# Experts in the order of their loads, with a slot count for each place, in a fused attention and mixture-of-experts kernel

## The chip, the core and the metric

The kernel runs on one core of one Trainium2 chip. The metric is the device time of one execution in microseconds (us), told as the median of three runs. A profile of one further execution shows the instructions of five engines: TensorE (PE for matmuls and transposes, PEld for its weight loads), VectorE (DVE), ScalarE (ACT), GpSimd (POOL) and SyncE (SP), which issues most DMAs. DMAs move data between DRAM and SBUF; matmuls write to PSUM, which has eight banks of 128 partitions by 512 fp32 numbers.

## The reference

All data are fp32. There are S = 2048 tokens of D = 448 features, H = 16 heads of 28, E = 8 experts with F = 1792 hidden features, and every token takes the two experts with the largest logits.

```python
def _A_ref(x, wqkv, wo):                       # attention
    q, k, v = (x @ wqkv).reshape(B, S, 3, H, Dh).transpose(2, 0, 3, 1, 4)
    p = softmax(einsum("bhqd,bhkd->bhqk", q, k) * Dh ** -0.5)
    return einsum("bhqk,bhkd->bhqd", p, v).transpose(0, 2, 1, 3).reshape(B, S, D) @ wo

def _B_ref(x, w_gate, w1, w2):                 # experts
    logits = x @ w_gate
    topk_idx = argsort(-logits)[:, :2]
    gates = softmax(take_along_axis(logits, topk_idx))
    out = 0
    for e in range(E):
        w = (gates * (topk_idx == e)).sum(-1, keepdims=True)
        out = out + w * (silu(x @ w1[e]) @ w2[e])
    return out

g = sigmoid((x * gate_w).sum(-1, keepdims=True))
return g * _A_ref(x, wqkv, wo) + (1 - g) * _B_ref(x, w_gate, w1, w2)
```

The inputs are random numbers with a spread of 0.05. How many tokens an expert gets (its load) is known only once the logits are computed. A load is about 512 on average (4096 choices over 8 experts).

## The kernel before

**Precision.** Each fp32 factor of a large product is split into a high half that TensorE takes in one pass (type fp32r) and a low half, the remainder; a product is the sum of high x high, high x low and low x high. ScalarE writes the high half as a copy, and VectorE or GpSimd subtracts it for the low one. The 448 features are four blocks of rows: three of 128, and a fourth of 64 rows that holds high and low halves together. So a product over the features takes 3 x 3 + 2 = 11 matmuls.

**Stages.** (1) After `BUSY` = 20 transposes of the identity (L338) with which PE begins, the value stage (to L388) goes through sixteen tiles of 128 tokens: PE makes the values and the logits of a tile, ScalarE copies the values to `v_s` (L376), and SP stores them in DRAM (L382). From the fifth tile on it also stores blocks of zeros from SBUF (`zf`) to `ys_d` (L385, L388): 24 blocks for spilled slots and one for the tail of each expert, 32 in all. (2) The query and key stage: `qk_tile` (L558) makes a block of 128 features of queries or keys for four chunks of 512 tokens; ScalarE copies the result to `hi` (L578), DVE subtracts (L581), SP stores both halves (L582, L583). Between DVE's pieces of this work stand those of `routing` (L397), a generator: top-two choice, each token's rank in its expert by matmuls with a triangle of ones (L431 to L433), the slot of each choice, and the lists `idx_i` (which token sits in a slot), `spill_i`, `cnt_i` (the loads) and `coef`. Four blocks come before the last piece of the routing, then three more (5, 2, 6); ahead of these three, the tokens of the first expert are gathered (`gather`, L202, an indirect DMA of GpSimd) and its first three weight tiles loaded (`load_w1`, L214, three DMAs each on SP). (3) The experts, L834 to L950. (4) Attention proper, L1040 on, whose exponentials run on ScalarE, then the output projection with the experts' rows gathered from `ys_d`.

**Slots.** Every expert has `CAP` = 576 slots, four tiles of 128 and a fifth of 64, and `CPAD` = 640 rows of `ys_d`. Tokens beyond 576 go to spill tiles of 128, which a loop at the end (L752) works off if there are any. Experts are taken in the order 0 to 7.

**Inside an expert.** The hidden features go in two halves (`hf`) of seven blocks. In the up layer each block is made for two halves of the columns (`HC` = 288 slots), 11 matmuls each (L870), so a half expert has 154 of them. ScalarE applies silu from PSUM: once to `hh` (the high half), once to `hf32` for GpSimd's low half (L749), and to `ht` for the fifth tile. In the second layer (L920) a tile of 128 slots takes 21 matmuls of 448 columns; before the four tiles stands the fifth (`last_slots`, L794), in a branch (L904) that is taken where the load is over 512. The first half's result waits in `ysb`, the second adds to it and stores to `ys_d`. Weights: SP loads `w1` (`load_w1`) and `w2` (`fetch_w2`) some tiles ahead; ScalarE splits off the high halves (L696, L734), GpSimd the low ones (L702, L740). `turn_x` (L718) transposes the next expert's gathered tokens, in the second halves.

**The score-maximum stream.** Attention needs each row's largest score. PE computes the scores for it among the experts' matmuls, in steps of six banks (`max_stream`, L91; matmuls L106, VectorE's reductions L126), and seven where the spare one of the two accumulator banks is lent (L120). The function `worked(ns, due, bank)` is called after every matmul of the experts with its length as the author reckons it. A step is emitted where a position is due: five dues in a half's up layer, six in the second halves of the last four experts, one at the fifth tile, and one in each of the four tiles.

```python
w1_due = [(18, 46, 73, 100, 128), (11, 35, 59, 83, 107, 131)]   # matmul of 0..153
W2_DUE = [(15, 13, 12, 10), (16, 14, 13, 12)]                    # matmul of 1..21, by tile
free = due <= i < due + 4 and (n_k > 1 or not turns)             # a bank may be lent
```

A finished maximum of four query tiles is transposed on PE and stored (`store_max`, L141), where a bank is free.

**Who sets the order.** PE, VectorE and ScalarE, and GpSimd too in the experts, run in the order in which the code is written. The order of SP's DMAs is made by a planner, which places them by its own estimate of when they can go; it is not the written one. For example, keys for the attention (L638), written in the seventh expert, are issued at 160.7 us, in the first.

## Time and profile before

| what | us |
| --- | --- |
| three runs | 1445.17, 1443.89, 1442.52 |
| median | 1443.89 |
| the profiled execution, its own time | 1443.26 |
| its span, first to last instruction | 1441.4 |
| PE busy / PEld busy | 1423.7 / 953.7 |
| DVE / ACT / POOL busy | 794.5 / 899.2 / 646.5 |
| expert stage | 121.8 to 913.9 |

How to read it: times count from the start of the span. In a row of busy time, `L870 PE MATMUL acc<-xeh,w1h 128*128 128x288` is a matmul of line 870 with the tile `xeh` as its input and `w1h` as its other one, into `acc`, over 288 columns. `[2.47 <-DVE dl L424]` says that the engine stood idle for 2.47 us before this instruction, and that what ended it was VectorE's write of `dl` on line 424. A row of waits, `ACT v_s L376 <- DMA v_d<-v_s: 14.1, 8, 4.6`, gives who waited for whom, then the total in us, how often, and the longest one. The granted clock is the share of its full clock that TensorE was given; it is 1.00 in all of this profile. PE's busy times overlap one another, so a matmul's cost is read from the distance between starts.

### The profile page before, as it was taken

The numbers are of one execution on the slowest core, as the hardware profiler recorded it, in microseconds if no ns is written. First come the engines' busy times: TensorE is split into PE (matmuls) and PEld (weight loads), VectorE is DVE, ScalarE is ACT, GpSimd is POOL, SyncE is SP. The second block draws the span as 40 slices with busy tenths as digits, with TensorE's granted clock in tenths as the row PEclk, the third lists the DMA queues.
The fourth block names the chain that finished last, engine by engine and source line by source line (L and its number), as shares of the span: only waits on it lengthen the run. The fifth ranks groups of instructions, "written<-read, shape, count | busy, mean of one in ns | idle before, by whom it ended". The sixth has DMA issues, their size and how long they took to land. (4 is left out here: it accounts for less than half of the span.)

```text
span 1441.4 us, 28118 instructions
## 1 busy us (share of the span) xinstructions
PE 1423.7 (99%) x11025; PEld 953.7 (66%) x11025; DVE 794.5 (55%) x858; ACT 899.2 (62%) x1559; POOL 646.5 (45%) x685
## 2 busy tenths in 40 slices
PE   9999999999999999999999999999999999999998
PEld 8788888888888888788888887533333333333347
DVE  5636777777778778778688787111142111221136
ACT  5235355344443553453444434799999999999981
POOL 1124597577666874874775656212222112112110
PEclk9999999999999999999999999999999999999999
DMA  9887532344133323331431320311422231142103
GB/s 332 291 289 238 169 112 78 97 136 129 43 103 118 103 81 110 123 98 55 137 118 37 107 70 3 108 47 49 130 55 59 78 98 47 43 122 64 32 20 119
DMA packets 110201, 153.18 MB, mean 106 GB/s; under 512 B 17884, under 2 KB 81516, under 8 KB 110064
## 3 DMA queue, kind: packets, MB, share of 16 engines
q1 hardware_dynamic: 100832, 129.86, 28.7%
q0 software_dynamic: 9088, 21.22, 4.9%
q8 instruction: 90, 1.47, 0.4%
q14 instruction: 47, 0.39, 0.1%
q10 hardware_dynamic: 144, 0.23, 0.1%
HBM read 109.20 MB, written 37.85 MB: 102 GB/s over the span
## 5 line engine op out<-in xcount | busy, mean ns | idle before, releaser
L126 DVE TENSOR_REDUCE mp<-pm 128x2 f32<-128x1024 f32 (+2 forms) x324 | 552.3, 1747 | 130.8 <-PE pm L106 130.3
L1058 ACT ACTIVATE P<-ps 128x1536 f32<-128x1536 f32 x254 | 367.9, 1448 | 0.0
L1067 PE MATMUL po<-P,V 128*32 128x512 f32 x2032 | 270.6, 604 | 0.0
L870 PE MATMUL acc<-xeh,w1l 128*128 128x288 f32 x880 | 258.5, 301 | 0.0
L870 PE MATMUL acc<-xeh,w1h 128*128 128x288 f32 x880 | 256.6, 298 | 0.0
L667 PEld LDWEIGHTS ps<-Q,Kh 29*128 29x128 f32 x2032 | 77.8, 183 | 212.6 <-ACT P L1057 212.3
L740 POOL TENSOR_TENSOR w2l<-w2r,w2h 128x448 fp32r<-128x448 f32 x112 | 129.0, 1153 | 168.9 <-ACT w2h L734 168.9
L870 PE MATMUL acc<-xel,w1h 128*128 128x288 f32 x660 | 195.1, 296 | 0.0
L667 PE MATMUL ps<-Q,Kh 29*128 29x512 f32 x2032 | 190.0, 444 | 0.0
L872 ACT ACTIVATE hh<-acc 128x288 fp32r<-128x288 f32 x224 | 92.3, 412 | 154.1 <-PE acc L870 154.1
L870 PEld LDWEIGHTS acc<-xeh,w1l 128*128 128x128 f32 x880 | 165.9, 189 | 18.6 <-issue 18.6
L920 PE MATMUL acc<-w2h,hh 128*128 128x448 f32 x448 | 171.8, 383 | 0.0
L870 PEld LDWEIGHTS acc<-xeh,w1h 128*128 128x128 f32 x880 | 165.7, 188 | 9.0 <-issue 7.3
L920 PE MATMUL acc<-w2l,hh 128*128 128x448 f32 x448 | 167.2, 373 | 0.0
L920 PE MATMUL acc<-w2h,hl 128*128 128x448 f32 x448 | 165.0, 368 | 0.0
L702 POOL TENSOR_TENSOR w1l<-w1r,w1h 128x512 fp32r<-128x512 f32 (+1 forms) x88 | 137.5, 1563 | 43.5 <-ACT w1h L696 25.3
L1071 DVE COPY osb<-po 128x512 f32<-128x512 f32 x16 | 11.1, 691 | 264.7 <-PE po L1067 246.9
L1014 POOL DMA_DIRECT2D sum_d<-osb x64 | 32.2, 515 | 271.7 <-DVE osb L1071 238.4
L1057 ACT ACTIVATE P<-ps 128x512 f32<-128x512 f32 x254 | 151.7, 597 | 1.4 <-ACT P L1058 0.5
L749 POOL TENSOR_TENSOR hl<-hf,hh 128x512 fp32r<-128x512 f32 x112 | 143.4, 1287 | 0.0
L106 PE MATMUL pm<-khg,qg 28*128 28x512 f32 x969 | 118.2, 454 | 9.7 <-DVE mp L126 5.9
L870 PEld LDWEIGHTS acc<-xel,w1h 128*128 128x128 f32 x660 | 124.6, 189 | 3.1 <-issue 2.9
(203 smaller groups left out, 1881.3 us busy)
## 6 DMA issues: line engine op xcount, KB each, us to landing
w2r<-in_w_dram SPq DMA_DIRECT2D x112, 224.0 KB
w1r<-in_w_dram SPq DMA_DIRECT2D x56, 384.0 KB
ys_d<-zf SPq DMA_DIRECT2D x32, 224.0 KB
qkh_d<-hi SPq DMA_DIRECT2D x28, 256.0 KB
qkl_d<-lo SPq DMA_DIRECT2D x28, 256.0 KB
w1r<-in_w_dram SPq DMA_DIRECT2D x112, 64.0 KB
ys_d<-yo SPq DMA_DIRECT2D x32, 224.0 KB
v_d<-v_s SPq DMA_DIRECT2D x16, 256.0 KB
```

The source lines that it names most:

```text
L106: nc.tensor.matmul(banks[n], qgs[g, qt // 4][rw, (qt % 4) * 128:(qt % 4 + 1) * 128], kh[g, kc][rw], start=True, stop=True)
L126: nc.vector.tensor_reduce(mp[:, (o + lo) % 256:(o + lo) % 256 + hi - lo], pm[:, lo:hi], axis=AX.X, op=ALU.max)
L667: nc.tensor.matmul(banks[j], k[rw, ks], q[rw, c], start=i == 0, stop=i == 2)
L702: nc.gpsimd.tensor_tensor(l[:, :, half], r[:, :, half], h[:, :, half].bitcast(F32), op=ALU.subtract)
L740: nc.gpsimd.tensor_tensor(w2l, w2r, w2h.bitcast(F32), op=ALU.subtract)
L749: nc.gpsimd.tensor_tensor(hl, hf32, hh[:, 0:512].bitcast(F32), op=ALU.subtract)
L870: nc.tensor.matmul(pu[:, 0:HC], a, b[:, cs], start=i == 0, stop=i == len(mms) - 1)
L872: nc.scalar.activation(hh[:, cs], pu[:, 0:HC], AF.Silu)
L920: nc.tensor.matmul(py[:n, 0:D], a[:, cs], b, start=i == 0, stop=i == 3 * NH - 1)
L1057: nc.scalar.activation(P[:, 0], p1, AF.Exp, scale=SCALE)
L1058: nc.scalar.activation(P[:, 1:4], p3, AF.Exp, scale=SCALE)
L1067: nc.tensor.matmul(po[32 * j:32 * j + 32], v[:, kt % 8, 32 * j:32 * j + 32], P[:, j] if n > 1 else P[j], start=kt == 0, stop=kt == NT - 1)
```

## The change

Three things are changed together, with what they need.

**Order and slots.** The routing ranks the experts by load: `key` = 8 x load − number, `pos` = how many experts have a larger key, so place 0 is the fullest. Slots, index lists, loads (`cnt_i`, now two rows: the load and the expert's number by place) and the loop over experts go by place. Place p has `CAPS[p]` = 576 − 12 p slots, at least 512: 576, 564, 552, 540, 528, 516, 512, 512, and `HC` half of that. `CTS` holds the tile sizes; the last two places have no fifth tile and no branch. Weights are addressed by a register that holds the number of the place's expert (`experts`, read from `cnt_i` on SP in `load_experts`, ahead of the first weight tiles). Tokens over a place's capacity go to spill tiles as before.

**Zeros.** The 32 stores of `zf` in the value stage are gone. One block of zeros is stored to DRAM (`zero_d`), and in the first half of each expert, after each of the four tiles of the second layer, a copy from `zero_d` to `ys_d` is written on SP, DRAM to DRAM.

**Positions.** `worked` now stores a finished maximum whenever a bank is offered, not only where a step is due; `W2_DUE` is later by up to two matmuls, and `free` opens earlier. `BUSY` is 15 instead of 20. The evacuation of a fifth tile is done for the two row groups apart, over its own number of slots.

```diff
-BUSY = 20
+BUSY = 15
...
-CT = [128, 128, 128, 128, CAP - 512]
-HC = CAP // 2
+CAPS = [max(CAP - 12 * p, 512) for p in range(E)]
+CTS = [[128] * 4 + [c - 512] * (c > 512) for c in CAPS]
...
+    zero_d = dram.tile([128, D], F32, name="zero_d")
...
-    cnt_i = consts.tile([128, E], I32, name="cnt_i")
+    cnt_i = consts.tile([128, 2, E], I32, name="cnt_i")
...
     def worked(ns, due=False, bank=None):
         hold[0] = max(0, hold[0] - ns)
         want[0] += due
-        if want[0] and not hold[0]:
-            if flush and bank:
-                store_max(*flush.pop(0), bank())
-                hold[0] = STORE_NS
-                return
+        if not hold[0] and flush and bank:
+            store_max(*flush.pop(0), bank())
+            hold[0] = STORE_NS
+        elif want[0] and not hold[0]:
             if bank:
                 spare.append(bank())
             next(ms, None)
...
     def gather(e, k):
+        n = CTS[e][k]
         xg = pe.tile([128, 512], F32, name="xg", bufs=5)
         nc.gpsimd.indirect_dma_start(
-            out=xg[:CT[k], 0:D], out_offset=None, in_=x,
-            in_offset=bass.IndirectOffsetOnAxis(ap=idx_i[:CT[k], 5 * e + k:5 * e + k + 1], axis=0))
+            out=xg[:n, 0:D], out_offset=None, in_=x,
+            in_offset=bass.IndirectOffsetOnAxis(ap=idx_i[:n, 5 * e + k:5 * e + k + 1], axis=0))
...
-    def load_w1(e, c):
+    w1f = w1.rearrange("e d f -> (e d) f")
+    w2f = w2.rearrange("e f d -> (e f) d")
+    experts = []
+    def load_experts():
+        for p in range(E):
+            experts.append(nc.values_load(cnt_i[0:1, 1, p:p + 1], engines=[mybir.EngineType.SP],
+                                          min_val=0, max_val=E - 1))
+    def load_w1(p, c):
         t = pe.tile([128, 4, 256], F32, name="w1r", bufs=3)
-        rows4(t, w1[e][:, c * 256:(c + 1) * 256], nc.sync)
+        cs = slice(c * 256, (c + 1) * 256)
+        nc.sync.dma_start(t[:, 0:3], w1f[ds(experts[p] * D, 384), cs].rearrange("(b p) n -> p b n", p=128))
+        for r in (0, 64):
+            nc.sync.dma_start(t[r:r + 64, 3], w1f[ds(experts[p] * D + 384, 64), cs])
...
         nc.gpsimd.memset(zf, 0.0)
+        nc.gpsimd.dma_start(zero_d, zf)
...
             nc.sync.dma_start(v_d[ts], v_s.rearrange("p h d -> p (h d)"))
-            if t >= 4:
-                for i in range(2 * t - 8, 2 * t - 6):
-                    nc.sync.dma_start(ys_d[NMAIN + i * 128:NMAIN + (i + 1) * 128], zf)
-                    if i % 3 == 0:
-                        r0 = (i // 3 + 1) * CPAD
-                        nc.sync.dma_start(ys_d[r0 - CPAD + 512:r0], zf)
...
-            nc.vector.tensor_copy(cnt_i, rk[:, NT])
+            cnt = rk[:, NT]
+            key = tmp("key", [128, E])
+            nc.vector.scalar_tensor_tensor(key, cnt, float(E), io8[:, 0], op0=ALU.mult, op1=ALU.subtract)
+            yield
+            EE = [128, E, E]
+            ahead = tmp("ahead", EE)
+            nc.vector.tensor_tensor(ahead, bc(key.unsqueeze(1), EE), bc(key.unsqueeze(2), EE), op=ALU.is_gt)
+            yield
+            pos = tmp("pos", [128, E])
+            nc.vector.tensor_reduce(pos, ahead, axis=AX.X, op=ALU.add)
+            yield
+            cap = tmp("cap", [128, E])
+            nc.vector.tensor_scalar(cap, pos, -12.0, float(CAP), op0=ALU.mult, op1=ALU.add)
+            nc.vector.tensor_scalar(cap, cap, 512.0, None, op0=ALU.max)
+            yield
+            nc.vector.tensor_tensor(key, cnt, cap, op=ALU.subtract)
...
+            at = tmp("at", EE)
+            nc.vector.tensor_tensor(at, bc(pos.unsqueeze(1), EE), bc(io8[:, 0].unsqueeze(2), EE), op=ALU.is_equal)
+            yield
+            pc = tmp("pc", [128, 2, E])
+            for i, what in enumerate((cnt, io8[:, 0])):
+                nc.vector.tensor_tensor(ahead, at, bc(what.unsqueeze(1), EE), op=ALU.mult)
+                yield
+                nc.vector.tensor_reduce(pc[:, i], ahead, axis=AX.X, op=ALU.add)
+                yield
+            nc.vector.tensor_copy(cnt_i, pc)
...
         next(ms)
+        load_experts()
         xgs = [gather(0, k) for k in range(5)]
         w1rs = [load_w1(0, c) for c in range(3)]
...
-                nc.sync.dma_start(t, w2[i // NF][(i % NF) * 128:(i % NF + 1) * 128])
+                nc.sync.dma_start(t, w2f[ds(experts[i // NF] * FF + i % NF * 128, 128)])
...
-            n, w = CT[4], D // 2
+            n, w = CTS[e][4], D // 2
             py = accumulator()
             for f in range(NH):
                 w2r = w2t[e * NF + hf * NH + f][2]
                 for c in range(2):
-                    nc.tensor.matmul(py[64 * c:64 * c + n, 0:w], hs[f][2], w2r[:, c * w:(c + 1) * w],
+                    nc.tensor.matmul(py[64 * c:64 * c + n, 0:w], hs[f][2][:, 0:n], w2r[:, c * w:(c + 1) * w],
                                      start=f == 0, stop=f == NH - 1)
-            if hf == 0:
-                nc.scalar.activation(y[:, 0:w], py[:, 0:w], AF.Copy)
-                return
             r0 = e * CPAD + 512
-            yo = sb.tile([128, D], F32, name="yo")
-            nc.scalar.activation(yo[:, 0:w], py[:, 0:w], AF.Copy)
-            nc.gpsimd.tensor_tensor(yo[:, 0:w], yo[:, 0:w], y[:, 0:w], op=ALU.add)
+            yo = sb.tile([128, D], F32, name="yo") if hf else y
             for c in range(2):
-                nc.gpsimd.dma_start(ys_d[r0:r0 + n, c * w:(c + 1) * w], yo[64 * c:64 * c + n, 0:w])
+                rw = slice(64 * c, 64 * c + n)
+                nc.scalar.activation(yo[rw, 0:w], py[rw, 0:w], AF.Copy)
+                if hf:
+                    nc.gpsimd.tensor_tensor(yo[rw, 0:w], yo[rw, 0:w], y[rw, 0:w], op=ALU.add)
+                    nc.gpsimd.dma_start(ys_d[r0:r0 + n, c * w:(c + 1) * w], yo[rw, 0:w])
...
-        W2_DUE = [(15, 13, 12, 10), (16, 14, 13, 12)]
+        W2_DUE = [(15, 14, 13, 12), (16, 15, 14, 13)]
         for e in range(E):
-            cnt = nc.values_load(cnt_i[0:1, e:e + 1], min_val=0, max_val=S)
+            CT, HC = CTS[e], CAPS[e] // 2
+            later = CTS[e + 1] if e + 1 < E else []
+            if len(CT) == 5:
+                cnt = nc.values_load(cnt_i[0:1, 0, e:e + 1], min_val=0, max_val=S)
...
-                    hh = sb.tile([128, CAP], F32R, name="hh", bufs=8)
+                    hh = sb.tile([128, 512], F32R, name="hh", bufs=8)
                     hf32 = sb.tile([128, 512], F32, name="hf32", bufs=3)
-                    ht = sb.tile([128, CAP - 512], F32, name="ht", bufs=8)
+                    ht = sb.tile([128, CAP - 512], F32, name="ht", bufs=8) if len(CT) == 5 else None
                     for c in range(2):
                         cs = slice(c * HC, (c + 1) * HC)
                         pu = accumulator()
                         for i, (a, b) in enumerate(mms):
                             nc.tensor.matmul(pu[:, 0:HC], a, b[:, cs], start=i == 0, stop=i == len(mms) - 1)
                             worked(U_NS, 2 * NM * f + c * NM + i in w1_due[six])
-                        nc.scalar.activation(hh[:, cs], pu[:, 0:HC], AF.Silu)
+                        nh = min(HC, 512 - c * HC)
+                        nc.scalar.activation(hh[:, c * HC:c * HC + nh], pu[:, 0:nh], AF.Silu)
                         if c == 0:
                             nc.scalar.activation(hf32[:, 0:HC], pu[:, 0:HC], AF.Silu)
                             for i in w2_now:
                                 split_w2_high(i)
                         else:
-                            nc.scalar.activation(hf32[:, HC:512], pu[:, 0:512 - HC], AF.Silu)
-                            nc.scalar.activation(ht, pu[:, 512 - HC:HC], AF.Silu)
+                            nc.scalar.activation(hf32[:, HC:512], pu[:, 0:nh], AF.Silu)
+                            if ht:
+                                nc.scalar.activation(ht[:, 0:CT[4]], pu[:, nh:HC], AF.Silu)
...
-                        with tc.If(cnt > 512):
-                            last_slots(e, hf, hs, ysb[4])
+                        if len(CT) == 5:
+                            with tc.If(cnt > 512):
+                                last_slots(e, hf, hs, ysb[4])
                         worked(0, True)
...
-                            free = due <= i < due + 4 and (n_k > 1 or not turns)
+                            free = (12 if turns else 10) <= i < due + 4 and (n_k > 1 or not turns)
                             worked(Y_NS, i == due, other_accumulator if free else None)
...
+                    if hf == 0 and n_k:
+                        r0 = e * CPAD + 512 if n_k == 1 else NMAIN + (3 * e + n_k - 2) * 128
+                        nc.sync.dma_start(ys_d[r0:r0 + 128], zero_d)
```

More of the change, by code (lines that the diff above doesn't have):

```diff
@@ L228, in x_tile @@
     def x_tile(xg, k, new_pt, xeh, xel):
-        n = CT[k]
+        n = CTS[0][k]
         flush_x()
@@ L928, in tile_gated_mha_moe @@
                             j = n_k if f == 1 and n_k > 1 else f // 4
-                            turn_x(xgs[j], j, xeh, xel)
+                            if j < len(later):
+                                turn_x(xgs[j], j, later[j], xeh, xel)
+                    if hf == 0 and n_k:
+                        r0 = e * CPAD + 512 if n_k == 1 else NMAIN + (3 * e + n_k - 2) * 128
+                        nc.sync.dma_start(ys_d[r0:r0 + 128], zero_d)
                     if hf == 0:
```

41 lines of the change are left out of this document (18 added, 23 removed).

## The prediction

> **What bounds the kernel now.** First the page's head and its DMA lines, then the busy time by stretch: columns are the stretch in us, its length, the busy time of PE, PEld, DVE, ACT and POOL, the granted TensorE clock, the DMA share and GB/s.
>
> ```profile
> span 1441.4 us, 28118 instructions
> ...
> ys_d<-zf SPq DMA_DIRECT2D x32, 224.0 KB
> ...
> 5.60:47.00 41.40, 41.29 (x193) 35.63 (x191) 21.77 (x58) 21.68 (x42) 2.78 (x33) 1.00 1.01 368
> ...
> 121.80:913.90 792.10, 782.28 (x5180) 653.32 (x5179) 598.62 (x460) 359.63 (x945) 523.50 (x457) 1.00 0.32 100
> ...
> 1100.00:1400.00 300.00, 299.95 (x3145) 104.01 (x3144) 68.72 (x121) 298.96 (x315) 56.85 (x93) 1.00 0.23 64
> ```
>
> There are three regimes. The value stage (5.6 to 47) fills PE and DMA at once. The experts (121.8 to 913.9) are PE's, with DVE at 76% beside it. From 915 ScalarE's exponentials set the pace, and the change touches nothing there. So the change is priced in the first two.
>
> In the experts PE's timeline gives what one matmul costs. Its busy column overlaps neighbours, so the starts are read (start, duration, engine, line, tile, shape, count).
>
> ```profile
> 422.82 0.30 PE L870 MATMUL acc<-xeh,w1h 128*128 128x288 f32 x1
> ...
> 426.27 0.29 PE L870 MATMUL acc<-xeh,w1l 128*128 128x288 f32 x1
> 426.50 0.73 PE L106 MATMUL pm<-khg,qg 28*128 28x512 f32 x6
> ...
> 427.39 0.29 PE L870 MATMUL acc<-xel,w1h 128*128 128x288 f32 x1
> ```
>
> ```profile
> 154.71 0.36 PE L920 MATMUL acc<-w2l,hh 128*128 128x448 f32 x1
> ...
> 158.15 0.37 PE L920 MATMUL acc<-w2h,hh 128*128 128x448 f32 x1
> ```
>
> Between 422.82 and 426.27 lie 26 starts: 132.7 ns a matmul of 288 columns. Between 154.71 and 158.15 lie 17: 202.4 ns for 448. The line through both is p(N) = 7 ns + 0.436 ns per column. A step of the score-maximum stream (L106) costs PE 427.39 − 426.27 − 2 × 0.133 = 0.86 us.
>
> The second clock in this stage is VectorE, which must reduce each step's six PSUM banks before the next step may write them.
>
> ```profile
> 568.48 0.73 PE L106 MATMUL pm<-khg,qg 28*128 28x512 f32 x6 [0.18 <-issue]
> 572.81 0.50 PE L106 MATMUL pm<-khg,qg 28*128 28x512 f32 x4 [0.22 <-DVE mp L126]
> ```
>
> ```profile
> 569.25 3.42 DVE L126 TENSOR_REDUCE mp<-pm 128x4 f32<-128x2048 f32 x2 [0.78 <-PE pm L106]
> ```
>
> ```profile
> PE pm L106 <- DVE mp L126: 5.9, 22, 0.6
> ```
>
> 0.77 us after the step's first matmul DVE starts, it takes 3.42, and PE goes on at 4.33 to 4.34 from step to step. That is a floor. In halves with five dues (28 or 27 matmuls apart) the interval is 28 × 0.1327 + 0.86 = 4.58 and the floor isn't felt. In the second halves of the last four experts, with six dues 24 apart, it is 4.04, so PE waits 0.30, five times each: 4 × 1.5 = 6.0, which is the 5.9 us of that last row.
>
> **The narrower experts.** The eight places get 576, 564, 552, 540, 528, 516, 512 and 512 slots. The reference's own inputs give loads of 561, 545, 514, 507, 501, 500, 497 and 471, so every token fits and no spill tile runs. Each place has 308 up matmuls over half its slots. The columns saved are 0, 6, 12, 18, 24, 30, 32 and 32, together 154: 308 × 154 × 0.436 ns = 20.7 us. The line is drawn below its two points; at worst the time stays at 132.7 (a rival below), and I take the line because the time per column is nearly the same at both points (0.461 and 0.452 ns).
>
> Much of it DVE takes back. With N = 276, 270, 264, 258 and 256 the four intervals of a five-due half fall below 4.34 by 0.08, 0.22, 0.47, 0.76 and 0.86 in all (for 256: p = 118.8 ns, 28p + 0.86 = 4.19, 27p + 0.86 = 4.07). Places 2 and 3 have two such halves, places 4 to 7 one: 3.6 us. A six-due half is pinned to 5 × 4.34 whatever N is, so its waits grow from 5.9 to 12.1 in all: 6.2. A step that also uses the spare accumulator has seven banks, and DVE is done with them 4.6 us after its first matmul:
>
> ```profile
> 158.45 0.50 PE L106 MATMUL acc<-khg,qg 28*128 28x512 f32 x1
> 158.98 0.69 DVE L120 TENSOR_REDUCE mp<-acc 128x1 f32<-128x512 f32 x1 [1.06 <-PE acc L106]
> 159.59 3.41 DVE L126 TENSOR_REDUCE mp<-pm 128x3 f32<-128x1536 f32 x2
> ```
>
> The branch at a fifth tile and its evacuation, by line (min, median, max in ns):
>
> ```profile
> L904 PEldq COMPARE_BRANCH  x22: 70/193/334, 144.7 to 891.3; - x22
> L803 ACT ACTIVATE ysb<-acc x3: 358/358/359, 149.5 to 641.6; 128x224 f32<-128x224 f32 x3
> ```
>
> W2_DUE now lets the last step of a second layer fall two or one matmuls later, so 9 × 0.2024 + 11p + 0.86 = 4.0 us are left before the first step of a six-due half: 4 × 0.6 = 2.4 waited. The run-up from the last due to the step at the fifth tile is 26 or 23 matmuls, 0.86 and a branch of 0.19: for places 4 to 7 it falls short by 0.1, 0.2, 0.4, 0.4 and by 0.5, 0.5, 0.75, 0.6, together 3.4 against 4 × 0.24 today: 2.4. On the other side the steps inside a second layer now lie 20 × 0.2024 + 0.86 = 4.9 apart, where in each first half one interval of 16 matmuls (4.1, short by 0.5) becomes one of 15 behind six banks (short by 0.34): −1.2 over eight. Together 3.6 + 6.2 + 2.4 + 2.4 − 1.2 = 13.4 go back.
>
> Four branches (two halves of places 6 and 7) vanish at 0.19: 0.8. Two turns of a fifth tile vanish, eight short transposes: 0.5. Three experts ran the fifth tile before (x3) and three do after. Its evacuation becomes two ScalarE copies, 0.36 more each time behind PE's next accumulator; ScalarE is busy 360 of 792 us there: nothing, at worst 6 × 0.36 = 2.2. The hidden layer loses 28 or more ScalarE copies, off PE's path. POOL at 523 of 792 us has its deadlines a pair of blocks later and covers its part. New worked() stores a finished maximum earlier and doesn't delay the step: the number of dues, and so of steps, stays. Experts: 20.7 + 0.8 + 0.5 − 13.4 = 8.6 us saved.
>
> **The zeros and SP's order.** Now the value stage.
>
> ```profile
> 12.06 0.34 SPq L385 DMA_DIRECT2D ys_d<-zf  x1
> ...
> 14.61 1.00 SPq L382 DMA_DIRECT2D v_d<-v_s  x2
> ...
> 160.70 1.37 SPq L638 DMA_DIRECT2D Kh<-qkh_d  x1
> ```
>
> ```profile
> ACT v_s L376 <- DMA v_d<-v_s: 14.1, 8, 4.6
> ```
>
> ```profile
> 49.04 0.39 PE L569 MATMUL pq<-xl,wqk_h 128*128 128x512 f32 x1
> 51.90 0.22 PE L431 MATMUL pt<-mb,tri 128*128 128x136 bf16 x1 [2.47 <-DVE dl L424]
> ```
>
> Thirty-two stores of 224 KB are 7.3 MB, 20 us of the 368 GB/s. They stand in the rings before the value stores, ScalarE waits for value buffers (14.1 us), the logits come late, and PE stands still from 49.27 to 51.90: 2.6 us. If the zeros leave this stage, those are won. But SP's order isn't the written one: a zero block written for token tile 4 left at 12.06, before the first value store, and keys written in the seventh expert left at 160.7, in the first. The new copies wait only for one small store, so in SP's gaps they can be drawn forward in time to where the old zeros were. I take that: no gain, 0. The ends are −2.6 (they leave) and the price of rival B. In the experts themselves, DMA's 0.32 share hides them.
>
> **The first weights.** Weight loads now need registers, and these need the routing's last result.
>
> ```profile
> L835 SPq TENSOR_LOAD <-cnt_i x8: 263/368/713, 121.6 to 172.6; - x8
> L835 SPq FUSED_REGOPS  x8: 147/153/192, 122.1 to 173.2; - x8
> ```
>
> ```profile
> 93.05 6.54 SPq L212 DMA_DIRECT2D w1r<-in_w_dram  x9
> 99.69 0.53 SPq L582 DMA_DIRECT2D qkh_d<-hi  x1
> 102.75 0.60 ACT L578 ACTIVATE hi<-pq 128x512 fp32r<-128x512 f32 x1 [7.75 <-DMA qkh_d<-hi]
> 104.24 0.50 PE L569 MATMUL pq<-xh,wqk_h 128*128 128x512 f32 x1
> 157.20 1.56 SPq L212 DMA_DIRECT2D w1r<-in_w_dram  x3
> ```
>
> Behind the nine first weight copies SP holds the store of a query block; ScalarE waits 7.75 us for it, and PE's next free accumulator is the one that this activation reads: 102.75 + 0.60, DVE's 0.69 behind it, and PE starts at 104.24. So what SP is given before 99.69 lands on PE. Eight register loads at 0.37 + 0.15 are 4.2; nine copies with an address to compute, at one register operation each, 1.4. Part of the 5.6 comes back: SP waits for data between the stores before 93, and a slower issue leaves less in the rings ahead of the store, which landed 3.0 after its issue. I take half, 2.8 us lost. Bounds: 0, if the order puts the loads into gaps, and 4.2 + 9 × 0.5 = 8.7 if an address doubles the issue (1.56 / 3 = 0.52); a gain is excluded, as SP only gets work. Later register addresses lie in SP's idle time.
>
> **Small edits.** From the timelines of DVE, ScalarE and PE:
>
> ```profile
> 66.70 0.69 DVE L581 TENSOR_TENSOR lo<-pq,hi 128x512 fp32r<-128x512 f32 x1 [1.28 <-ACT hi L578]
> ...
> 110.46 0.83 ACT L157 ACTIVATE xg<-xg 128x64 f32<-128x64 f32 x5
> ```
>
> The routing gets some thirteen more short DVE operations, which lie in gaps like the 1.28 us of the first of these rows; its index list comes one slot (1 us) later, while the gathers' first reader, at 110, waits for nothing. POOL's added store of zeros meets a POOL that is busy 2.8 of 41.4 us. All three: 0.
>
> ```profile
> 1.41 4.53 PE L339 MATMUL pt<-ident 128*128 128x128 f32 x20 [1.41 <-DVE ident L266]
> ...
> 6.12 0.40 PE L334 MATMUL pq<-xeh,xl 128*128 128x458 f32 x1
> 6.36 0.37 PE L334 MATMUL pq<-xel,xh 128*128 128x458 f32 x1
> 6.58 0.19 PEld L334 LDWEIGHTS pq<-xeh,xh 128*128 128x128 f32 x1 [0.24 <-ACT xeh L325]
> ```
>
> Five warm-up transposes fewer (BUSY) end PE's first run at 4.5 instead of 5.5, but at 6.58 it waits for the next weight block either way: 0. [...]
>
> **The sum.** −8.6 + 0 + 2.8 = −5.8. The profiled execution took 1443.26 us, with 1.9 outside its span; the median shown is 0.6 above it. 1443.26 − 5.8 = 1437.5; half a microsecond is added for the median: 1438.
>
> **Rivals.** A: the zeros do leave the value stage, and the register loads fall into gaps. −8.6 − 2.6 = −11.2: 1432.1. The written order speaks for it, the row at 160.7 against.
>
> B, the slower end: the copies are drawn into the value stage and a copy from DRAM to DRAM holds the rings longer than a store from SBUF. That stage is full (share 1.01), so each extra microsecond of ring time moves the logits and PE's stall. If a copy takes the rings for a read and a write at the stage's 368 GB/s, twice a store's time, the extra is 20 us: 1457.5; halfway, at 1.5 times, 10 us: 1447.5. It decides from 1.3 times (5.8 us). No row has such a copy; for it speaks that it reads and writes the same memory, against it that greedy filling may spread them further. [...]
>
> C: the first weights cost their full 8.7 and eat the experts' gain: 1443.4, no change.
>
> D: the change does not shorten matmuls: the pace at 256 columns stays at 132.7 because a weight load, not the stream, sets it. Then 1.3 remain against 2.8: 1444.8. The falling time from 448 to 288 speaks against it.
>
> **Chances.** Forecast 0.42, A 0.20, B 0.22, C 0.10, D 0.06. About 0.2% (2.9 us) can be told from no change. Forecast and A are faster: 0.62; C and D the same: 0.16; B slower: 0.22. The range runs from 1430, 2 us below A, past B's middle, 1450; the forecast alone, with the first weights between 0 and 6, holds 1434 to 1441.
>
> **What would show it.** L870's starts 118 to 119 ns apart at 256 columns (D if not); PE's wait for DVE in L106's row at some 17 to 19 us instead of 5.9 (if it stays at 6, the experts give 20 and I am too cautious); the copies' issue times on SP before 50 (forecast, B) or in the experts (A), and PE's stall before L431 near 2.6, far above or gone; the store after the first weights some 3 us later than now against its data, and PE with a hole of that size near 104. A late w2 or w1 tile behind SP's new work would make it wrong in a way that no row here prices.

## The result, and the profile after

The changed kernel takes 1475.08 us (median of five runs, 1473.47 to 1477.23) where the kernel before takes 1443.89: 1.0215 times as long, 95% interval 1.0201 to 1.0229. The forecast was 1438, with a range up to 1450. The page's head, and its row of busy engines:

```profile
span 1473.2 us, 28645 instructions
...
PE 1417.5 (96%) x11012; PEld 947.1 (64%) x11012; DVE 796.0 (54%) x871; ACT 886.6 (60%) x1531; POOL 646.0 (44%) x682
```

PE is busy 6 us less than before, and the span is 32 us longer: PE stands still. Where, the busy time by stretch tells (columns as in the prediction: PE, PEld, DVE, ACT and POOL, then the granted clock, the DMA share and GB/s):

```profile
300.00:500.00 200.00, 198.76 (x1367) 165.19 (x1366) 151.10 (x118) 91.41 (x251) 141.44 (x128) 1.00 0.33 101
500.00:700.00 200.00, 186.37 (x1232) 154.54 (x1231) 150.98 (x117) 83.69 (x228) 126.98 (x112) 0.97 0.32 96
700.00:900.00 200.00, 178.30 (x1155) 147.92 (x1154) 143.50 (x113) 74.51 (x179) 114.15 (x97) 0.97 0.27 84
```

The kernel before has there:

```profile
300.00:500.00 200.00, 199.25 (x1328) 166.76 (x1324) 151.10 (x117) 91.58 (x241) 137.93 (x122) 1.00 0.33 102
500.00:700.00 200.00, 196.83 (x1310) 163.54 (x1309) 153.25 (x118) 89.86 (x237) 134.91 (x119) 1.00 0.32 99
```

Between 300 and 500 the changed kernel gets more matmuls done (1367 against 1328) at full clock. From 500 on PE stands 14 to 22 us of each 200, and the clock's mean is 0.97 instead of 1.00. What it stands for, in the waits of PE in the experts (us in total, times, the longest):

```profile
PE acc L144 <- DVE mg L137: 27.5, 8, 3.7
PE pm L108 <- DVE mp L128: 14.5, 35, 0.8
PE acc L108 <- DVE mr L146: 2.0, 4, 0.6
```

The first row is new. Line 144 is the transpose in `store_max`; `mg` is the finished maximum of four query tiles. One of the eight, in PE's timeline and then VectorE's:

```profile
170.80 0.49 PE L108 MATMUL acc<-khg,qg 28*128 28x512 f32 x1
170.80 0.73 PE L108 MATMUL pm<-khg,qg 28*128 28x512 f32 x6
171.47 0.47 PE L955 MATMUL acc<-w2h,hh 128*128 128x448 f32 x1
175.62 0.38 PE L144 MATMUL acc<-ident,mg 128*16 128x128 f32 x1 [3.69 <-DVE mg L137]
175.65 0.72 PE L955 MATMUL acc<-w2l,hh 128*128 128x448 f32 x1
176.17 0.57 PE L955 MATMUL acc<-w2h,hl 128*128 128x448 f32 x1
176.55 0.57 PE L955 MATMUL acc<-w2h,hh 128*128 128x448 f32 x1
```

```profile
171.33 0.69 DVE L122 TENSOR_REDUCE mp<-acc 128x1 f32<-128x512 f32 x1 [0.89 <-PE acc L108]
171.94 3.41 DVE L128 TENSOR_REDUCE mp<-pm 128x3 f32<-128x1536 f32 x2
175.38 0.18 DVE L137 TENSOR_REDUCE mg<-mp 128x4 f32<-128x16 f32 x1
```

A step of seven banks is emitted, one matmul of the second layer follows, and then comes the transpose of the maximum that this very step finishes. VectorE needs until 175.56 for the seven banks and for `mg`. PE runs in written order, so all matmuls behind the transpose wait with it: the next one starts at 175.65, 4.18 us after the last one ahead of it. Sixteen maxima are stored in all; eight of them end in a step of the up layers or at the fifth tile, where no bank is offered, and are stored in the next second layer without a wait. Behind the wait the matmuls are also slow: 176.17 to 176.55 is 0.38 us for one, where it was 0.20. The granted clock, by stretches of 2 us:

```profile
172.00:174.00 2.00, 0.00 (x0) 0.00 (x0) 2.00 (x3) 0.00 (x0) 0.00 (x0) 1.00 0.40 107
...
176.00:178.00 2.00, 2.00 (x7) 1.78 (x6) 0.28 (x1) 0.00 (x0) 0.00 (x0) 0.50 0.15 21
178.00:180.00 2.00, 2.00 (x9) 1.87 (x8) 0.00 (x0) 0.68 (x2) 0.00 (x0) 0.50 0.29 102
...
182.00:184.00 2.00, 2.00 (x17) 1.47 (x16) 0.60 (x1) 0.86 (x4) 1.07 (x1) 1.00 0.93 353
```

The clock goes to half at 174.7, in the 3.7 us without a matmul, and is back at 1.00 from 181.5, some 6 us after their end. The eight second layers with such a wait are 3.6 to 5.2 us longer than those without one (26.0 instead of 21.0 us in the first), 36.5 in all, and the up layers behind them 2.2 longer: 38.7 us. The experts run from 124.1 to 946.4, 822.3 us; without the 38.7 it would be 783.6, against 792.1 before, near the 8.6 us that were forecast as the experts' gain. That is a subtraction; the runs test it.

### The profile page after: what moved, and what is told of

Same layout as the page of the kernel before. It is cut to its first block, busy times and chain, and to the rows that moved or that the text cites. A ratio compares the mean times of both kernels' runs of the same rounds, so it can differ in the third digit from the quotient of the medians.

```text
span 1473.2 us, 28645 instructions
## 1 busy us (share of the span) xinstructions
PE 1417.5 (96%) x11012; PEld 947.1 (64%) x11012; DVE 796.0 (54%) x871; ACT 886.6 (60%) x1531; POOL 646.0 (44%) x682
## 5 line engine op out<-in xcount | busy, mean ns | idle before, releaser
L902 PE MATMUL acc<-xeh,w1l 128*128 128x256 f32 (+6 forms) x880 | 251.3, 295 | 0.0
L902 PE MATMUL acc<-xeh,w1h 128*128 128x256 f32 (+6 forms) x880 | 249.6, 292 | 0.0
L902 PE MATMUL acc<-xel,w1h 128*128 128x256 f32 (+6 forms) x660 | 191.4, 290 | 0.0
L905 ACT ACTIVATE hh<-acc 128x256 fp32r<-128x256 f32 (+6 forms) x224 | 86.2, 385 | 155.9 <-PE acc L902 152.0
L955 PE MATMUL acc<-w2h,hh 128*128 128x448 f32 x448 | 175.2, 391 | 0.0
L955 PE MATMUL acc<-w2l,hh 128*128 128x448 f32 x448 | 171.1, 382 | 0.0
L955 PE MATMUL acc<-w2h,hl 128*128 128x448 f32 x448 | 170.1, 380 | 0.0
L108 PE MATMUL pm<-khg,qg 28*128 28x512 f32 x969 | 118.2, 454 | 16.5 <-DVE mp L128 14.5
```

Of the source, the lines that this page charges most:

```text
L108: nc.tensor.matmul(banks[n], qgs[g, qt // 4][rw, (qt % 4) * 128:(qt % 4 + 1) * 128], kh[g, kc][rw], start=True, stop=True)
L902: nc.tensor.matmul(pu[:, 0:HC], a, b[:, cs], start=i == 0, stop=i == len(mms) - 1)
L905: nc.scalar.activation(hh[:, c * HC:c * HC + nh], pu[:, 0:nh], AF.Silu)
L955: nc.tensor.matmul(py[:n, 0:D], a[:, cs], b, start=i == 0, stop=i == 3 * NH - 1)
```

## The experiments

Each time stands beside runs of the kernel before on the same chip; that kernel takes 1443 to 1449 us from chip to chip, so differences within a group of runs are read. Spans of the expert stage are from the first matmul of the up layer to the last one of the second layer.

| run | us | kernel before, same chip | ratio, 95% interval | expert stage, us |
| --- | --- | --- | --- | --- |
| e1_old_worked | 1434.42 | 1444.88 | 0.9921 (0.9899 to 0.9944) | 125.4 to 906.2: 780.8 |
| e2_old_positions | 1473.74 | 1444.88 | 1.0203 (1.0180 to 1.0226) | 123.2 to 944.1: 820.9 |
| e3_before_new_worked | 1485.76 | 1444.88 | 1.0287 (1.0261 to 1.0312) | 122.3 to 954.5: 832.2 |
| e4_filled | 1461.52 | 1444.88 | 1.0115 (1.0092 to 1.0138) | 122.1 to 931.7: 809.6 |
| f1_late | 1442.18 | 1448.94 | 0.9951 (0.9938 to 0.9965) | 125.7 to 908.8: 783.1 |
| f3_late_lazy | 1435.47 | 1448.94 | 0.9905 (0.9890 to 0.9920) | 120.5 to 903.8: 783.3 |
| f4_late_cap576 | 1448.57 | 1448.94 | 0.9999 (0.9990 to 1.0008) | 123.5 to 915.4: 791.9 |
| g1_late_zeros_sbuf | 1444.35 | 1448.94 | 0.9964 (0.9951 to 0.9978) | 128.3 to 911.1: 782.8 |
| h1_old_worked_lazy | 1428.95 | 1443.30 | 0.9900 (0.9883 to 0.9916) | 119.2 to 900.4: 781.2 |
| h2_busy20 | 1429.08 | 1443.30 | 0.9906 (0.9889 to 0.9922) | 119.3 to 900.2: 780.9 |
| h3_six_first | 1428.51 | 1443.30 | 0.9899 (0.9882 to 0.9915) | 119.9 to 899.6: 779.7 |
| h4_filled12 | 1464.27 | 1443.30 | 1.0149 (1.0123 to 1.0175) | 124.7 to 935.6: 810.9 |

**Is it the early store?** Two theories: the place of the store (S), or the moved dues and the wider window (P). The first run takes worked() back, the second the positions, and the third puts the new worked() alone into the kernel before.

```diff
-        if not hold[0] and flush and bank:
-            store_max(*flush.pop(0), bank())
-            hold[0] = STORE_NS
-        elif want[0] and not hold[0]:
+        if want[0] and not hold[0]:
+            if flush and bank:
+                store_max(*flush.pop(0), bank())
+                hold[0] = STORE_NS
+                return
             if bank:
```

> The changed kernel with the function worked() of before: a finished maximum is stored only where a step is due, and the step follows three matmuls later. Theory S (the early store): in the changed kernel PE's transpose of a maximum stands right behind the step whose banks VectorE has still to reduce; eight of the sixteen maxima end in a step of a second layer with a bank on offer, and eight second layers are 3.6 to 5.2 us too long, 36.5 us in all, with 2.2 more in the up layers behind them at a lower clock. Expected 1475.1 - 38.7 = 1436.4 us (1433 to 1440), no wait of PE for mg, clock 1.00 in the experts. Theory P (the positions): the later dues and the wider window for the spare bank make the steps collide with VectorE, whatever worked() does. Expected about 1470 us, second layers of 26 us still there.

```diff
-        W2_DUE = [(15, 14, 13, 12), (16, 15, 14, 13)]
+        W2_DUE = [(15, 13, 12, 10), (16, 14, 13, 12)]
...
-                            free = (12 if turns else 10) <= i < due + 4 and (n_k > 1 or not turns)
+                            free = due <= i < due + 4 and (n_k > 1 or not turns)
```

> The changed kernel with the old W2_DUE and the old window for the spare bank; the new worked() stays. Theory S: the window still runs three matmuls past the step, so the same eight transposes stand right behind their steps: eight waits of about 3.7 us for mg, 1472 to 1480 us. Theory P: the cause is gone, about 1440 us.

The third run has the first diff the other way round, in the kernel before.

> The kernel before with the new worked() alone, nothing else changed. Theory S: the whole loss comes with it: 1443.9 + 38.7 = 1482.6 us (1476 to 1488), eight waits of PE for mg. Theory P: no loss, 1443.9 us within 2.

Measured: 1434.4, 1473.7 and 1485.8. PE's waits, first of the kernel with the old worked(), then of the kernel before with the new one:

```profile
PE pm L108 <- DVE mp L128: 16.2, 37, 1.1
```

```profile
PE acc L142 <- DVE mg L135: 27.6, 8, 3.7
PE pm L106 <- DVE mp L126: 5.3, 21, 0.5
```

With the old function no wait for `mg` is left in the second layers, and the time is 10.5 us below the kernel before instead of 31.2 above it. With the new function alone the kernel before gets the same eight waits, 27.6 us, and loses 40.9. The old positions change nothing of it (27.6, 8). Theory S holds, P falls. The experts begin at another time from kernel to kernel, between 122 and 125; the runs on the first weights come to that.

**The wait and the clock apart.** Here PE gets something to do while it waits.

```diff
-    def store_max(g, qc, mg, bank):
+    def store_max(g, qc, mg, bank, fill=0):
+        for _ in range(fill):
+            nc.tensor.transpose(bank[:, 0:128], ident, ident)
...
-            store_max(*flush.pop(0), bank())
+            store_max(*flush.pop(0), bank(), FILL if age[0] < 1000 else 0)
```

`age` counts the matmul time since the last step that finished a maximum; FILL is 24 in the first of these runs and 12 in the second.

> The changed kernel; ahead of each transpose of a maximum that stands right behind its step PE makes 24 transposes of the identity into the same bank, work that is thrown away, so that it isn't idle while it waits. Theory S with a clock share: the wait itself stays (27.5 us in eight waits), but the granted clock stays at 1.00 behind it, and the excess over the wait, 38.7 - 27.5 = 11 us, goes: 1464 us (1461 to 1468). If the lower clock has another cause than PE's idle time, the clock still falls to 0.5 behind the stores and the time stays at 1475 us or above.

> The changed kernel with 12 instead of 24 throw-away transposes ahead of a transpose that stands right behind its step, so that PE is idle for some 2.2 us there instead of 3.7 or 0.6. If the granted clock falls only behind longer idle times, it stays at 1.00 in the experts and the time is that of 24 transposes, 16.6 us above the kernel before (14 to 19). If 2.2 us are enough, it falls to 0.5 behind some or all of the eight, and the time lies between that and 30 us above the kernel before.

With 24 the experts take 809.6 us instead of 822.3. So of the 41.5 us between the changed kernel's stage and that of e1 (822.3 − 780.8) 12.7 were the price of the lower clock, where 11 were expected, and 28.8 are left for the waits (27.5 by the row above) and what else differs between the two kernels. The stretch from 500 to 700 of this run, and the same of the run with 12:

```profile
500.00:700.00 200.00, 191.05 (x1304) 158.68 (x1304) 153.89 (x120) 85.22 (x233) 130.80 (x115) 1.00 0.32 96
```

```profile
500.00:700.00 200.00, 188.89 (x1269) 156.70 (x1269) 152.98 (x118) 84.26 (x229) 128.78 (x114) 0.99 0.32 97
```

With PE kept busy (its longest wait for `mg` is 0.7 us) the clock is 1.00 there, where the changed kernel has 0.97: in this kernel its fall comes from the idle time. With 12 the waits are 13.9 us in eight, at most 2.0, and the experts take 810.9, within 1.3 of the run with 24. By stretches of 30 us from 560 to 920 the clock is 1.00 in all but the one from 650 to 680, where its mean is 0.94. This wait lies in it:

```profile
668.43 1.53 PE L146 MATMUL acc<-ident 128*128 128x128 f32 x12
671.98 0.28 PE L147 MATMUL acc<-ident,mg 128*16 128x128 f32 x1 [2.02 <-DVE mg L138]
...
673.16 0.57 PE L962 MATMUL acc<-w2h,hh 128*128 128x448 f32 x1
673.54 0.57 PE L962 MATMUL acc<-w2l,hh 128*128 128x448 f32 x1
```

The last two start 0.38 us apart, where two right behind the wait (672.50 and 672.70) start 0.20 apart.

The whole run is 21.0 us above the kernel before, outside the 14 to 19 that were expected if the clock held, and 4.3 more than the one with 24 (16.6); 2.6 of that is the later begin of its experts, 124.7 against 122.1.

**A store that is early, but not too early.** The store is taken whenever a bank is offered, once 4 us of matmuls have gone by since the step.

```diff
+        age[0] += ns
-        if not hold[0] and flush and bank:
+        if not hold[0] and flush and bank and age[0] > LATE_NS:
...
+            had = len(flush)
             next(ms, None)
+            if len(flush) > had:
+                age[0] = 0
```

> The changed kernel; worked() stores a finished maximum whenever a bank is offered, but only once 4 us of matmuls have gone by since the step that finished it. Theory S: no transpose waits for VectorE any more; beside the kernel with the old worked() the steps are no longer put off by three matmuls where a store comes first. 1434.4 us, that kernel's time, or up to 2 less (1431 to 1436). If storing early is bad in itself (a bank or VectorE's copy taken at a bad place), 1440 or more.

The wait is gone, but the expectation of a time at or below that of the old worked() is missed: 6.8 us below the kernel before, where the old worked() gave 10.5 on its own chip. Of the difference 2.3 us show in the experts, 783.1 against 780.8, and 1.9 of them as a wait that the old function doesn't have:

```profile
PE pm L109 <- DVE mp L129: 16.2, 37, 1.1
...
PE acc L109 <- DVE mr L147: 1.9, 4, 0.6
```

A store just ahead of a step takes the bank that the step borrows, and PE waits until VectorE has copied the transposed maximum out of it. The remaining 1.4 us stay open; they stand between runs on two chips, on which the kernel before differs by 4.1 us.

**The narrower experts alone.** All places get 576 slots again; the rest is f1_late.

```diff
-CAPS = [max(CAP - 12 * p, 512) for p in range(E)]
+CAPS = [CAP for p in range(E)]
...
-            nc.vector.tensor_scalar(cap, pos, -12.0, float(CAP), op0=ALU.mult, op1=ALU.add)
+            nc.vector.tensor_scalar(cap, pos, 0.0, float(CAP), op0=ALU.mult, op1=ALU.add)
```

> f1_late with 576 slots at every place (the order by load, zeros, registers and positions stay; two places get their fifth tile and branch back). Prices the narrower experts alone. By the prediction's sum 20.7 us of columns, 0.8 of branches and 0.5 of turns come back, and VectorE gives back its waits of 3.6, 6.2 and about 2.4 for the run-ups: f1_late + 9.8 (8 to 12). If VectorE's floor takes nothing back, f1_late + 20 and PE's wait for mp stays as it is; if matmuls of 256 columns are no faster than those of 288, f1_late + 1.

The time rises by 6.4 us, less than the 8 to 12 that were expected. The experts alone take 791.9 instead of 783.1: 8.8 us, near the 9.8 of the sum. In the whole time less of it shows, since the wide kernel's experts begin 2.2 us earlier (PE's hole at the first weights is 2.7 us there and 3.9 in f1_late). PE's wait for VectorE in the wide kernel:

```profile
PE pm L109 <- DVE mp L129: 2.9, 6, 1.0
```

against the 16.2 above: 13.3 us go back to VectorE's floor. The columns' 20.7, with 0.8 for branches and 0.5 for turns, less 13.3 are 8.7, against 8.8 measured. The forecast had 13.4 for what goes back, counting the moved positions in.

**The first weights.** Only the first expert's number goes into a register ahead of the first weight tiles.

```diff
     def load_experts():
-        for p in range(E):
+        if len(experts) < E:
+            p = len(experts)
             experts.append(nc.values_load(cnt_i[0:1, 1, p:p + 1], engines=[mybir.EngineType.SP],
...
     def load_w1(p, c):
+        while len(experts) <= p:
+            load_experts()
```

(and the same two lines in `fetch_w2`, with `i // NF` for `p`.)

> f1_late, but only the first expert's number is loaded into a register ahead of the first weight tiles; each other one where its expert's weights are first fetched. Theory R (the registers): in the changed kernel SP spends 87.6 to 93.8 us on eight register loads (6.2 us, seven of them 0.57 to 0.9 apart), and the store that PE's accumulator hangs on goes out that much later. With one load 4 us of it go: PE's hole near 104 shrinks from 2.7 or more to under 1, and the experts begin near 120 instead of 124: 3 to 4.5 us less than f1_late. Rival: SP waits for the routing's last result (cnt_i) and not for the loads; then the first weights go out when they did and the time stays within 1 of f1_late.

In the changed kernel, the register loads, SP's first weights, the store behind them, and PE:

```profile
L218 SPq TENSOR_LOAD <-cnt_i x8: 262/268/1452, 87.6 to 93.3; - x8
```

```profile
94.01 0.44 SPq L224 DMA_DIRECT2D w1r<-in_w_dram  x1
...
100.51 0.53 SPq L614 DMA_DIRECT2D qkh_d<-hi  x1
```

```profile
101.90 0.39 PE L601 MATMUL pq<-xh,wqk_l 128*128 128x512 f32 x1
105.01 0.50 PE L601 MATMUL pq<-xh,wqk_h 128*128 128x512 f32 x1 [2.73 <-DVE lo L613]
```

In f3_late_lazy, SP:

```profile
91.25 1.26 SPq L234 DMA_DIRECT2D w1r<-in_w_dram  x2
...
97.12 1.01 SPq L622 DMA_DIRECT2D qkh_d<-hi  x1
```

The store goes out at 97.1 instead of 100.4 in f1_late (100.5 in the changed kernel), PE has no hole there any more, where f1_late has one of 3.9 us, and the experts begin at 120.5 instead of 125.7. The time falls by 6.7 us, more than the 3 to 4.5 expected. A part that wasn't in the expectation is likely the clock. In kernels with eight loads it is 0.50 for 3.4 us at the hole in the changed kernel (2.7 us idle), e2 (2.5) and f4 (2.7), and for 6.8 in e1 (4.0); in e4 (2.7) it is 1.00 from 101 to 113. In f3_late_lazy the matmuls start 0.23 us apart from 96.8 to 105.9, as in the changed kernel at a clock of 1.00.

**The zeros.** Stores from SBUF in the value stage as before, no copies; the rest is f1_late.

```diff
+            if t >= 4:
+                for i in range(2 * t - 8, 2 * t - 6):
+                    nc.sync.dma_start(ys_d[NMAIN + i * 128:NMAIN + (i + 1) * 128], zf)
...
-                        nc.sync.dma_start(ys_d[r0:r0 + 128], zero_d)
```

> f1_late with the zeros stored from SBUF in the value stage, as before, and no copy inside the experts. In the changed kernel the copies were drawn into the value stage (13.6 us on), and yet PE's stall ahead of the rank matmuls (2.5 us) is gone and these come 2.1 us earlier. If that gain is the zeros' (their order among the value stores), the stall is back and the time is f1_late + 2 (1 to 3.5). If it is the routing's or the schedule's, it is f1_late within 1.

2.2 us slower than f1_late, as expected. The stall ahead of the rank matmuls is back, where the changed kernel has none; first the run's row, then PE at that place in the changed kernel:

```profile
PE pt L443 <- DVE dl L436: 1.8, 1, 1.8
```

```profile
49.37 0.39 PE L601 MATMUL pq<-xl,wqk_h 128*128 128x512 f32 x1
49.82 0.22 PE L433 MATMUL pt<-mb,tri 128*128 128x136 bf16 x1
```

So the gain is that of the copies against the stores. SP's copies, its last store of values in the kernel before and after, and ScalarE's wait for such stores after:

```profile
L969 SPq DMA_DIRECT2D ys_d<-zero_d x32: 488/540/638, 13.6 to 183.4; - x32
```

```profile
50.08 0.49 SPq L382 DMA_DIRECT2D v_d<-v_s  x1
```

```profile
45.09 0.33 SPq L390 DMA_DIRECT2D v_d<-v_s  x1
...
179.30 4.63 SPq L969 DMA_DIRECT2D ys_d<-zero_d  x7
```

```profile
ACT v_s L384 <- DMA v_d<-v_s: 9.1, 6, 3.9
```

The planner did draw the copies into the value stage, from 13.6 us on, but 25 of them (before, 30 of the stores went out ahead of 50 us); the other seven come at 179 to 183 us. The last values go out 5.0 us earlier, and ScalarE's wait is 9.1 instead of 14.1 us. Seven copies less are 1.6 MB, 4.3 us at the stage's 368 GB/s. What of the gain is due to the seven and what to the order of the others wasn't told apart.

**Putting it together.** The next three kernels add: both repairs (the old worked(), one register load); 20 warm-up transposes; and six-due halves at the wide places.

> The changed kernel with the old worked() and with one register load ahead of the first weights (the others where an expert's weights are first fetched). If the two repairs add up: 10.5 us below the kernel before from the one and 6.7 from the other, 17 us below the kernel before on the same chip (14 to 19). If the hole in the first weights is only moved, 11 below.

> The kernel with both repairs and 20 warm-up transposes again instead of 15. In the changed kernel the first matmuls of the value stage start 0.54 and 0.39 us apart, where before 0.24, and the thirteenth starts at 10.11 us instead of 9.08. If that carries on, the time is 1.0 below the kernel with 15 (0.5 to 1.7); if the DMAs of that stage set its end anyway, it is the same within 0.5.

```diff
-                six = hf == 1 and e >= E - 4
+                six = hf == 0 and e < 3
```

> The kernel with both repairs and 20 transposes, with the six-due halves moved from the second halves of the last four experts to the first halves of the first three, where the columns are wide. A six-due half takes 26.7 us at any width, since VectorE's floor pins it; a five-due half took 24.6, 24.3 and 23.8 at the first three places and 23.4, 23.1, 23.3 and 23.9 at the last four. So the six-due halves cost 2.1 + 2.4 + 2.9 = 7.4 instead of 3.3 + 3.6 + 3.4 + 3.7 = 14: up to 6.6 below the kernel that they are moved in (2 to 7, since other steps of the stream come later where these come earlier). Rival: the floor is the stage's whole time, not the halves': the same number of steps then takes the same time, and nothing is won (within 1).

With both repairs the time is 1428.95 us, 14.4 below the kernel before, at the lower end of the 14 to 19 expected, where the changed kernel was 31.2 above it. It beats both. The warm-up changes nothing (1429.08). Neither do the moved six-due halves (1428.51), where 2 to 7 were expected. PE's wait for `mp` does fall, from 16.3 to 9.4 us, and the up layers get 4.2 us shorter, but the second layers get 4.2 longer, 2.5 of these in the last one. There the transpose of the last maximum now stands behind the first scores of the attention, and PE waits 1.6 us until ScalarE has emptied the bank. In number that is the rival of the expectation. Its mechanism isn't shown, since a floor of the whole stage would have kept the wait for `mp`; the rest of what took the gain back stays open.

## Why the prediction was wrong, step by step

**The step that failed** is one sentence: "New worked() stores a finished maximum earlier and doesn't delay the step". The steps were indeed not delayed. But a maximum counts as finished in the code when its last step is emitted, and VectorE is done with it only later. The prediction had the numbers: DVE starts 0.77 us after the step's first matmul and takes 3.42, PE is through with the step after 0.86. With the 0.18 of `mg` a transpose right behind the step waits 0.77 + 3.42 + 0.18 − 0.86 = 3.5 us; for seven banks and one matmul in between the trace shows 3.69. The old function could store only where a step was due, and the next due is 4 to 5 us on. The window, three matmuls longer than the due, offers a bank right behind each step of a second layer. In the sum this wait stood at nothing; the runs show 27.5 us of waits and, with the clock behind them, about 40. The edit was read for what it does to the queue of steps, and not for which engine makes the tile that the transpose reads, and when it is done. The rival on the slower side was put elsewhere (B, the copies).

**The clock** had no term. It added 12.7 us to what the waits alone cost. In the changed kernel half clock came with all eight waits for `mg`, seven of 3.55 to 3.69 us and one of 2.26, and in h4 with one of 2.02 us.

**The narrower experts**: right. Starts of matmuls at 256 columns, in the up layer of place 6:

```profile
738.06 0.28 PE L902 MATMUL acc<-xeh,w1l 128*128 128x256 f32 x1
...
740.70 0.28 PE L902 MATMUL acc<-xeh,w1l 128*128 128x256 f32 x1
```

22 matmuls apart: 120 ns, where 118.8 was forecast and rival D said 132.7. PE's wait for VectorE is 14.5 to 16.2 us, 17 to 19 were forecast. The stage without the early store comes to 783.6 by subtraction and 780.8 by e1, so 8.5 to 11.3 us saved against 8.6. One term of the sum has a slip that is smaller than this spread: 15 × 0.2024 + 0.86 is 3.90, short of 4.34 by 0.44 and not by 0.34, so that the −1.2 is −0.5 and the sum 7.9.

**The zeros**: the place was right for 25 of 32 copies, the size was not: 0 was taken, and 2.2 us are gained (g1), near the lower end of −2.6 that stood for all of them leaving. Rival B fell: the copies don't hold the rings longer in a way that any wait shows. With them the time is 2.2 us shorter than with the stores (f1 against g1), where B took 10 to 20 us more.

**The first weights**: the mechanism and the place were right (PE's hole at 105, the store behind the nine copies), and so was the size of the hole. Eight register loads took 6.2 us (87.6 to 93.8), where 4.2 was worked out; the nine copies took 6.4, as before, where 1.4 was added. So SP got 6.2 us more work, where 5.6 was worked out. The store went out at 100.51 instead of 99.69 while PE's matmuls ahead of the hole came 2.1 us earlier than before: 2.9 later against its data, so about half did come back, and the hole is 2.7 us, where 2.8 was forecast. But from these matmuls to the begin of the experts, 2.3 later than before, the loss is 4.4, within the bounds of 0 to 8.7. The 1.7 beyond the hole is half clock again: the granted clock is 0.50 from 106.4 to 109.8.

**The warm-up**: 0, and right, though not as argued:

```profile
1.42 3.46 PE L347 MATMUL pt<-ident 128*128 128x128 f32 x15 [1.42 <-DVE ident L276]
4.54 0.75 PE L342 MATMUL pq<-xeh,xh 128*128 128x458 f32 x1
5.08 0.59 PE L342 MATMUL pq<-xeh,xl 128*128 128x458 f32 x1
5.47 0.58 PE L342 MATMUL pq<-xel,xh 128*128 128x458 f32 x1
...
10.11 0.36 PE L342 MATMUL pq<-xeh,xh 128*128 128x458 f32 x1
```

The first three matmuls start 0.54 and 0.39 us apart, where before 0.53 and 0.24, and the thirteenth comes 1.0 us later (10.11 against 9.08); on the way the seventh waits 0.76 us for ScalarE. So 15 transposes leave more than the first of the matmuls slow, which is read from the pace alone: the record of the granted clock begins at 7.4 us here and at 6.2 before, and has nothing ahead of that. The stage makes the delay good, since h2 with 20 transposes isn't faster; that its DMAs are full either way is the likely reason, and not shown.

Without the early store the sum of these terms is −8.5 − 2.2 + 4.4 = −6.3 us, where −5.8 was forecast. That agreement is partly luck, as zeros and first weights miss in opposite ways. Run directly, the changed kernel without the early store is 10.5 us below the kernel before (e1, 8.1 to 14.6 by its interval) or 6.8 (f1): the forecast had the sign right and was, by e1, 4.7 too small, 2.7 of it in the experts.

## What to carry to other kernels

When an edit moves an instruction of an engine that runs in written order, look first at who produces its operand and when that engine is done; that the producer's instruction has been emitted says nothing. A wait on PE can cost more than its length: the granted clock fell to half with one wait of 2.02 us (h4) and with all eight of 2.26 to 3.69 us in the changed kernel, whose 27.5 us of waits cost about 40. And a change of several parts is best tried part by part: here one line cost four times what the others brought.

## What was not expected of the hardware

The granted clock and idle time: with 24 throw-away transposes, where the waits for `mg` in front of PE are at most 0.7 us, the clock is 1.00 in every stretch from 120 to 900 us (e4). With 12, one of the eight waits, of 2.02 us, has half clock behind it (h4); the others, 11.9 us together, show none. In the changed kernel all eight do, of 2.26 to 3.69 us.

The record of the clock also shows when it falls. In the changed kernel half clock begins at 106.4 us, behind the hole of 2.7 us, and at 174.7, 625.2, 673.0, 731.0, 782.2, 833.4, 884.6 and 932.4 us, with the eight waits. Four times it begins before the wait's end (by 0.4 to 2.1 us), four times behind it (by 0.1 to 0.8 us). It lasts 6.8 us at 174.7 and 673.0, and 3.4 us at each of the others. The kernel before has 1.00 up to 1439.7 us, and 0.50 in the last 1.6 us, where PE has no work. How long an idle time has to be for the fall can't be read from these: at the first weights 2.7 us brought half clock in the changed kernel and in f4, and none in e4.

In the changed kernel, register loads on SP start 0.56 to 0.91 us apart from the second on (0.27 for the load, 0.15 for the operation behind it, and the time between), and the load of the first alone took 1.45. Addresses from registers cost SP nothing that shows: nine copies took 6.4 us from the first to the last (94.01 to 100.41), and 6.54 without (from 93.05, in the kernel before).
